# Attention and MLP in one kernel: plain float32 for the product of the last two weights, and the memory term begun in the middle of a pair step

## Chip, cores and metric

One core of a Trainium2 chip runs the whole program. The metric is device microseconds of one execution; the time of a kernel is the median of several.

## What is computed

Two parts follow each other. Causal attention over 4 batches of 8 heads (576 positions, 64 wide) is mixed with the readout of a memory, and its result, 2304 tokens of 512, goes through an MLP that has no nonlinearity between its last two weights:

```python
a = softmax(causal(q @ k.T / 8))            # per batch and head
mem_out = (phi(q) @ M_prev) / (phi(q) @ z_prev + 1e-6)
x = g * mem_out + (1 - g) * (a @ v)          # phi(x) = elu(x) + 1, g = sigmoid(beta)
h = (x @ w1) * (x @ w2)                      # 512 -> 1024
out = (h @ w3) @ w_out                       # 1024 -> 1024 -> 512
```

The weights of the MLP arrive as 64-bit floats; the kernel reads them as pairs of 32-bit words and builds float32 from them.

## The kernel before

Since nothing stands between w3 and w_out, the kernel multiplies these two first (W = w3 @ w_out, 1024 x 512) and applies W to h. `w_gen` (L419) makes W in 8 blocks of 128 rows, each a sum over 8 chunks of 128. The operands are split in a high and a low part, both in the fast matmul form (float32r); each chunk is three matmuls of 512 columns: high x high, high x low, low x high. ACT copies a block's result as its high part (`wH`, L427), DVE takes the low part (`wL`, L405).

Every weight is converted by one of 40 jobs of 512 columns (`conv_stages`): 8 of w_out, 16 of w3, 16 of w1 and w2 (W12 below). The stages of a job: `load` (SP issues a DMA; below job 24 one DMA of 1 MB serves two jobs, L306, from there 0.5 MB for one, L315), `scale` (ACT, L322), `join` (two DVE instructions, L326 and L327), `split` (ACT copies the high part, L332; POOL subtracts for the low part, L333). `conv_tick` runs one stage of three jobs, one behind the other; `tick_ok` says whether a further job may start, by how much of W is done.

The attention works on pairs of heads, 16 of them, four to a batch. `pair_step(p)` issues the operations of one pair in the order of the list `ORDER`: t1 to t5 and th are transposes of the softmax of this pair (L236, L257; ACT copies them out of PSUM, L267), s and e are scores (PE L195, L209, with a DVE instruction for mask and maximum, L179) and exponentials (ACT L217) of the next pair, n their norm (DVE L221, L222, L226), lv, lqn and lq are loads (v; qn and z; q and k). The memory term of a pair is: `mem_a` (ma, two ACT instructions, L135, L136), `mem_b` (mb, DVE L141 and POOL L143), `mem_c` (mc, four small DVE instructions, L148 to L154, and POOL L156), all three for the next pair, then `mem_t` (mt, five transposes L162 into the PSUM tile x and an ACT copy), and `mem_mm` (mm, L273 and L274, plain float32), which leaves its sum in x; `pv_mm` (L283) adds to it, and `fin` (ACT L293, DVE L294) takes x out. There is one buffer each for qn, z, mt and x.

F in the list is a slot of filler for PE: `Fill.slot` runs one or two conversion ticks (two in the first 13 slots of a filler) and as many steps of the MLP as the plan of even shares asks for. In the first batch the filler is `w_gen`, in the others the MLP of the batch before (`gemm1`, L455, L461, L464, L466, L467; `gemm2`, L475, L480), and the MLP of the last batch runs alone at the end. The list is the order of priority; an engine's queue is filled by readiness and priority, so an instruction that is ready can be issued ahead of its place. Each queue runs in order.

Big SBUF tiles: eight slots r0 to r7 (raw weights in r0 to r3, split w_out in r4 to r7, later split W12 in all), a ring of four g0 to g3, seven x tiles (split w3 uses x4 to x6 in the first batch).

Of the kernel before, what the change touches and what calls it, by code (L numbers as in the profile page):

```python
# [8 lines left out]
F32 = mybir.dt.float32  # L9
F32R = mybir.dt.float32r  # L10
# [7 lines left out]


ORDER = (  # L20
    "lv lqn t1 F "
    "t2 F "
    "mt t3a F "
    "th t3b F "
    "s321 F "
    "e3 F "
    "n3 t4a F "
    "e2 e1 t4b t5 F "
    "n2 s4 F "
    "e4 F "  # L30
    "mm s0 e0 n4 F "
    "pv ma lq F "
    "fin mb mc F "
).split()


def f32(ap):
    return ap.bitcast(F32)
# [3 lines left out]
def attention_moe_kernel(  # L42
# [13 lines left out]
    nc = tc.nc  # L56
    B, H, D, _, S = qkt.shape
    DM = H * D
    NF = w12.shape[0]
    NC = DM // 128  # L60
# [9 lines left out]
    big = pool("big")  # L70
    ring = pool("ring")
# [6 lines left out]
    x_p = pool("x")  # L78
    a_p = pool("a", 2)
    o_p = pool("o", 2)  # L80
# [46 lines left out]
    def load_m(b):  # L127
        src = m_prev[b].rearrange("d (j t) e -> d t j e", t=2)
        for a in range(2):
            nc.sync.dma_start(out=md[64 * a:64 * a + 64, :, 64 * a:64 * a + 64], in_=src[:, a])  # L130
# [164 lines left out]


    def conv_stages(k, src, dh, dl):
        n = dh.shape[1]
        box = {}

        def load():
            if k < 24:
                if k % 2 == 0:
                    t = big.tile([128, 4 * n], F32, tag=f"r{k // 2 % 4}", name="wst")
                    raws[k // 2] = t.bitcast(U32).rearrange("p (j n w) -> p j n w", j=2, w=2)
                    nc.sync.dma_start(out=t.bitcast(U32), in_=src.bitcast(U32))  # L306
                box["raw"] = raws[k // 2][:, k % 2]
                return
            if k < 32:
                t = ring.tile([128, 3 * n], F32, tag=f"g{2 + k % 2}", name="wst")  # L310
                box["p"] = t[:, 2 * n:3 * n]
            else:
                t = x_p.tile([128, 2 * S], F32, tag=f"x{4 + k % 3}", name="wst")
            box["raw"] = t[:, 0:2 * n].bitcast(U32).rearrange("p (n w) -> p n w", w=2)
            nc.sync.dma_start(out=t[:, 0:2 * n].bitcast(U32), in_=src.bitcast(U32))  # L315

        def scale():
            if k < 24:
                box["p"] = ring.tile([128, n], F32, tag=f"g{k % 4}", name="wp")
            if k >= 32:  # L320
                box["p"] = o_p.tile([128, n], F32, tag="o", name="wp")
            nc.scalar.activation(out=box["p"], in_=f32(box["raw"][:, :, 1]), func=ACTF.Prelu, scale=2.0 ** -111, alpha=-(2.0 ** 32))  # L322

        def join():
            p = box["p"].bitcast(U32)
            nc.vector.tensor_scalar(out=p, in0=p, scalar1=3, scalar2=None, op0=ALU.logical_shift_left)  # L326
            nc.vector.scalar_tensor_tensor(  # L327
                out=p, in0=box["raw"][:, :, 0], scalar=29, in1=p, op0=ALU.logical_shift_right, op1=ALU.bitwise_or
            )

        def split():
            nc.scalar.activation(out=dh(), in_=box["p"], func=ACTF.Copy)  # L332
            nc.gpsimd.tensor_tensor(out=dl(), in0=box["p"], in1=f32(dh()), op=ALU.subtract)  # L333

        return load, scale, join, split

    big_t = {}

    def part(key, alloc, a, o, n):
        def get():  # L340
            if key not in big_t:
                big_t[key] = alloc()
            return big_t[key][:, a, o:o + n]
        get.shape = [128, n]
        return get

    conv_jobs = []
    raws = {}

    def add_job(src, key, alloc, o):  # L350
        conv_jobs.append(conv_stages(len(conv_jobs), src, part(key, alloc, 0, o, 512), part(key, alloc, 1, o, 512)))

    def whole(tag):
        return lambda: big.tile([128, 2, 1024], F32R, tag=tag, name="wsp")

    def w3_half(m):
        return lambda: x_p.tile([128, 2, S], F32R, tag=f"x{4 + m % 3}", name="w3s")

    for j in range(8):
        add_job(w_out[j // 2], ("wo", j // 2), whole(f"r{j // 2 + 4}"), 512 * (j % 2))  # L360
    for m in range(16):
        add_job(w3t[m // 2], ("w3", m), w3_half(m), 0)
    for j in range(16):
        add_job(w12[j // 2][:, 512 * (j % 2):512 * (j % 2) + 512], ("w12", j // 2), whole(f"r{j // 2}"), 512 * (j % 2))
    NJ = len(conv_jobs)
    tick = [0]
    nload = [0]
    w_done = [0]
    limit = [28]

    def tick_ok():
        k = tick[0]
        if 10 <= k < 26 and w_done[0] < k - 12:
            return False
        return k < limit[0] and (k < 32 or w_done[0] == 16)

    def load_upto(k):
        while nload[0] < min(k, NJ):
            conv_jobs[nload[0]][0]()
            nload[0] += 1  # L380

    def conv_tick():
        k = tick[0]
        tick[0] += 1
        if 0 <= k - 2 < NJ:
            conv_jobs[k - 2][3]()
        if 0 <= k - 1 < NJ:
            conv_jobs[k - 1][2]()
        if k < 24:
            load_upto(min(24, 8 + k // 2 * 2))  # L390
        else:
            load_upto(k + 2)
        if k < NJ:
            conv_jobs[k][1]()

    def conv_upto(k):
        while tick[0] <= k + 2:
            conv_tick()


    def w_gen():
        box = {}

        def low(i):
            nc.vector.scalar_tensor_tensor(  # L405
                out=wL[i], in0=box.pop(i), scalar=2.0 ** -16, in1=f32(wH[i]), op0=ALU.mult, op1=ALU.subtract
            )

        for i in range(NF):
            ps = ps_m.tile([128, DM], F32, tag="m", name="m")  # L410
            n = 0
            for kc in range(8):
                m = 2 * i + kc // 4
                if kc % 4 == 0:
                    conv_upto(8 + m)
                w = big_t["w3", m]
                wo = big_t["wo", kc // 2].rearrange("p a (k e) -> p a k e", k=2)[:, :, kc % 2]
                for a, b in ((0, 0), (0, 1), (1, 0)):
                    nc.tensor.matmul(ps, lhsT=w[:, a, 128 * (kc % 4):128 * (kc % 4) + 128], rhs=wo[:, b], start=(n == 0), stop=(n == 23))  # L419
                    n += 1  # L420
                if kc % 4 == 3:
                    w_done[0] += 1
                yield 648
                if kc == 0 and i:
                    low(i - 1)
            with tc.high_priority(100):
                nc.scalar.activation(out=wH[i], in_=ps, func=ACTF.Copy, scale=2.0 ** -16)  # L427
            box[i] = ps
        low(NF - 1)
# [55 lines left out]
    def moe_gen(b):  # L485
        for n in (2 * b, 2 * b + 1):
            yield from gemm1(n)
            while 128 * (done_g[0] + 1) <= U * (n + 1):
                yield from gemm2(done_g[0])
                done_g[0] += 1  # L490

    MOE_NS = 2 * NF * 8 * 366 + 9 * 0.5 * NF * 648
    W_NS = NF * 8 * 648


    class Fill:
# [6 lines left out]
        def slot(self):  # L503
            self.n += 1
            for _ in range(self.ticks if self.n > SLOTS else 2):
                if tick[0] <= NJ + 1 and tick_ok():
                    conv_tick()
            goal = self.lead * self.total * max(0, self.n - self.wait) / (self.slots - self.wait)
            while self.live and self.spent < goal:
                self.step()  # L510
# [11 lines left out]
    SLOTS = sum(t[0] == "F" for t in ORDER)  # L522
# [72 lines left out]
    for c in (3, 2, 1):  # L595
        s_exp(0, c)
        conv_tick()
# [12 lines left out]
    for b in range(B):  # L610
        load_m(b)
        if b == 0:
            F = Fill(w_gen(), W_NS, SLOTS * NC, wait=4)
        else:
            limit[0] = NJ + 2
            F = Fill(moe_gen(b - 1), MOE_NS, SLOTS * NC)
        for j in range(NC):
            pair_step(b * NC + j, F)
        F.finish()
    F = Fill(moe_gen(B - 1), MOE_NS, 1)  # L620
# [34 lines left out]
```

## Time and profile before

| | us |
|---|---|
| median of 3 runs | 605.61 (605.23 to 606.65) |
| the profiled execution | 605.53 |
| its span, first to last instruction | 603.7 |
| PE busy in the span | 554.7 (92%) |
| DVE busy | 310.9 (51%) |
| ACT busy | 294.0 (49%) |
| POOL busy | 161.8 (27%) |

Busy shares are means over stages of different kinds: the first batch of pair steps (18.9 to 144.4 us) computes W, the next three (144.4 to 522.4) run the MLP of the batch before as filler, and the rest is the MLP of the last batch alone. A stage is read by itself, with the granted clock of PE beside it (1.00 is 2.4 GHz, 0.50 is 1.2).

### The profile page before, as it was taken

Reading aid. Unit: us, or ns where it says so; the run is one execution under the profiler, and the core shown is the slowest. Engines: PE = TensorE matmul, PEld = TensorE weight load, DVE = VectorE, ACT = ScalarE, POOL = GpSimd, SP = SyncE. Lnnn points to the kernel's source line nnn. Section 1 sums busy time; section 2 is a strip of 40 time slices with the busy share of each in tenths; the row PEclk is TensorE's granted clock in tenths of the full one; section 3 lists DMA queues with packets and bytes.
Section 4 is the critical chain, followed back from the end, with each engine's and each line's share of the span. In section 5 each row is a group of like instructions: output and inputs, shape, how many; then the busy total and the mean of one; then the engine's idle time right before and its main releaser. Section 6 shows DMA issues by size and latency. Waiting matters only on the chain.

```text
span 603.7 us, 9527 instructions
## 1 busy us (share of the span) xinstructions
PE 554.7 (92%) x3504; PEld 455.7 (75%) x3504; DVE 310.9 (51%) x910; ACT 294.0 (49%) x747; POOL 161.8 (27%) x177
## 2 busy tenths in 40 slices
PE   4388889979789999999899989998999999999997
PEld 2255666757668788878787878777887889898996
DVE  5999687387882818172718172726435451111111
ACT  4776567575774445454545353515453644130210
POOL 1565144135653213121312031202120221031220
PEclk9879799989979999999999999999999999999999
DMA  7576321358522120203020302030213000000001
GB/s 277 210 274 234 97 68 27 90 174 241 171 87 71 38 88 5 86 23 111 10 82 25 102 5 84 25 108 27 64 28 99 22 23 1 36 1 17 18 2 52
DMA packets 23070, 48.32 MB, mean 80 GB/s; under 512 B 6896, under 2 KB 13040, under 8 KB 21488
## 3 DMA queue, kind: packets, MB, share of 16 engines
q1 hardware_dynamic: 23024, 47.72, 24.3%
q8 instruction: 27, 0.44, 0.3%
q14 instruction: 19, 0.16, 0.1%
HBM read 43.00 MB, written 4.72 MB: 79 GB/s over the span
## 4 chain that ended last, share of the span: by engine, by line
PE 58%; DVE 14%; issue 8%; DMA 7%; ACT 7%; POOL 5%; SPq 0%; DVEq 0%; POOLq 0%; ACTq 0%
PE m L455 26%; PE m L475 13%; PE x L283 5%; PE s L236 4%; PE s L195 4%; DMA qn<-qn 3%; PE m L419 3%; DMA wst<-w 3%; DVE sm L226 3%; DVE sm L179 2%; DVE wp L327 2%; POOL e L143 2%; ACT sm L217 2%; DVE wp L326 2%; POOL wsp L333 1%
## 5 line engine op out<-in xcount | busy, mean ns | idle before, releaser
L455 PE MATMUL m<-xs,wsp 128*128 128x288 f32 x1536 | 232.0, 302 | 9.9 <-DVE a L464 5.8
L455 PEld LDWEIGHTS m<-xs,wsp 128*128 128x128 f32 x1536 | 209.2, 189 | 19.8 <-DVE a L464 7.6
L467 POOL TENSOR_TENSOR ht<-a,ht 128x288 fp32r<-128x288 f32 (+2 forms) x96 | 57.4, 611 | 287.1 <-ACT ht L466 267.5
L217 ACT ACTIVATE sm<-sm,mx 128x448 f32<-128x448 f32 (+2 forms) x144 | 83.1, 578 | 71.3 <-DVE mx L179 71.1
L475 PE MATMUL m<-wH,ht 128*128 128x512 f32 x288 | 98.4, 402 | 0.0
L464 DVE SCALAR_TENSOR_TENSOR a<-m,a 128x288 f32<-128x288 f32 x64 | 29.1, 455 | 114.8 <-PE m L455 114.6
L267 ACT ACTIVATE pt<-s 128x512 f32<-128x512 f32 (+1 forms) x144 | 66.1, 484 | 34.4 <-PE s L236 26.9
L236 PE MATMUL s<-ident,sm 128*128 128x128 f32 x448 | 69.4, 282 | 8.6 <-DVE sm L226 6.4
L226 DVE TENSOR_SCALAR sm<-sm,sums 128x448 f32<-128x448 f32 (+2 forms) x144 | 74.5, 558 | 1.5
L195 PE MATMUL s<-raw 64*128 64x288 f32 (+3 forms) x320 | 60.7, 474 | 12.9 <-ACT pt L267 5.3
L236 PEld LDWEIGHTS s<-ident,sm 128*128 128x128 f32 x448 | 56.3, 145 | 14.1 <-issue 6.8
L179 DVE CUSTOM_DVE_ANT_0 sm<-s,mask 128x448 f32<-128x448 f32 (+2 forms) x144 | 59.3, 447 | 11.4 <-PE s L195 10.8
L475 PEld LDWEIGHTS m<-wH,ht 128*128 128x128 f32 x288 | 54.1, 188 | 13.2 <-issue 2.6
L195 PEld LDWEIGHTS s<-raw 64*128 64x128 f32 x320 | 32.3, 199 | 35.6 <-issue 11.2
L466 ACT ACTIVATE ht<-a 128x288 fp32r<-128x288 f32 (+2 forms) x96 | 31.4, 357 | 53.5 <-DVE a L464 53.4
L419 PE MATMUL m<-wsp,w3s 128*128 128x512 f32 x192 | 56.1, 426 | 0.7 <-POOL w3s L333 0.7
L475 PE MATMUL m<-wL,ht 128*128 128x512 f32 x144 | 56.3, 391 | 0.0
L283 PE MATMUL x<-pt,v 128*64 128x448 f32 (+4 forms) x384 | 46.7, 392 | 0.0
L461 ACT ACTIVATE a<-m 128x288 f32<-128x288 f32 x64 | 26.0, 407 | 40.8 <-PE m L455 35.0
L283 PEld LDWEIGHTS x<-pt,v 128*64 128x64 f32 x384 | 25.0, 137 | 24.1 <-issue 19.1
L419 PEld LDWEIGHTS m<-wsp,w3s 128*128 128x128 f32 x192 | 35.0, 198 | 10.7 <-issue 2.5
L143 POOL TENSOR_TENSOR e<-qn,z 128x640 f32<-128x640 f32 x16 | 25.4, 1589 | 34.9 <-DVE qn L141 34.0
(63 smaller groups left out, 498.0 us busy)
## 6 DMA issues: line engine op xcount, KB each, us to landing
raw<-qkt SPq DMA_DIRECT2D x16, 576.0 KB, 3.8
wst<-w3t SPq DMA_DIRECT2D x8, 1024.0 KB, 7.5
wst<-w SPq DMA_DIRECT2D x16, 512.0 KB, 4.5
qn<-qn SPq DMA_DIRECT2D x16, 320.0 KB, 2.9
v<-v SPq DMA_DIRECT2D x32, 160.0 KB, 2.4
out<-o SPq DMA_DIRECT2D x18, 256.0 KB, 2.0
wst<-w_out SPq DMA_DIRECT2D x4, 1024.0 KB, 9.7
z<-z_prev SPq DMA_DIRECT2D x16, 64.0 KB, 2.9
```

Source lines behind the costliest of these rows:

```text
L143: nc.gpsimd.tensor_tensor(out=e, in0=t, in1=zb, op=ALU.mult)
L179: nc.vector.tensor_tensor_reduce(out=sm[a][c][:, lo:hi] if c else sm0[:, 0:64], in0=x, in1=mask[:, S - KE[c] + lo:S - KE[c] + hi] if c els ...
L195: nc.tensor.matmul(x[:, o:o + hi - lo], lhsT=t[r, 0, 128 * c - 64:128 * c + 64], rhs=t[r, 1, lo:hi], start=True, stop=True)
L217: nc.scalar.activation(out=x, in_=x, func=ACTF.Exp, bias=mx, scale=-1.0, accum_out=sums_of(p)[:, k:k + 1])
L226: nc.vector.tensor_scalar(out=x, in0=x, scalar1=sums_of(p)[:, k:k + 1], scalar2=None, op0=ALU.mult)
L236: tr = lambda o, c, a, kc: nc.tensor.transpose(ps[:, o:o + 128], sm[a][c][:, 128 * kc:128 * kc + 128], ident)
L267: nc.scalar.activation(out=d, in_=s, func=ACTF.Copy)
L283: nc.tensor.matmul(x[64 * a:64 * a + 64, 384 + q0:384 + q1], lhsT=vv[:, a, kc], rhs=pt[:, a, o:o + q1 - q0], start=False, stop=(q0 == 0 or ...
L419: nc.tensor.matmul(ps, lhsT=w[:, a, 128 * (kc % 4):128 * (kc % 4) + 128], rhs=wo[:, b], start=(n == 0), stop=(n == 23))
L455: nc.tensor.matmul(ps[:, 0:U], lhsT=w[:, i, x, j], rhs=x_t[NC * b + j][:, xx, U * u:U * u + U], start=(k == 0), stop=(k == 11))
L467: nc.gpsimd.tensor_tensor(out=hbuf(f, 1)[:, p:p + c], in0=a[:, o:o + c], in1=f32(hbuf(f, 0)[:, p:p + c]), op=ALU.subtract)
L475: nc.tensor.matmul(ps, lhsT=hbuf(f, a)[:, p:p + 128], rhs=b[f], start=(k == 0), stop=(k == 23))
```

## The change

The operands of W are no longer split. `split` does nothing below job 24, and the scaled and joined value is written straight to its place. A chunk of W is one plain float32 matmul of 512 columns. The planned cost of a chunk goes from 648 to 870 ns; the filler starts at slot 4 in place of 5.

Unsplit w_out takes r4 and r5, so raw weights have six slots (r0 to r3, r6, r7) and are loaded 12 jobs ahead in place of 8. Unsplit w3 goes into the ring, one tile for a block. W12 jobs stage in x4 to x6 and in an output tile (before, jobs 24 to 31 staged in the ring). `tick_ok` lets W3 jobs run up to four blocks ahead.

In the list, mt goes from slot 3 to the start of a step, lqn from slot 1 to slot 2 (behind mt), ma from slot 12 to 5, mb from 13 to 6, mc from 13 to 9.

```diff
 ORDER = (
-    "lv lqn t1 F "
-    "t2 F "
-    "mt t3a F "
+    "lv mt t1 F "
+    "lqn t2 F "
+    "t3a F "
     "th t3b F "
-    "s321 F "
-    "e3 F "
+    "s321 ma F "
+    "e3 mb F "
     "n3 t4a F "
     "e2 e1 t4b t5 F "
-    "n2 s4 F "
+    "n2 s4 mc F "
     "e4 F "
     "mm s0 e0 n4 F "
-    "pv ma lq F "
-    "fin mb mc F "
+    "pv lq F "
+    "fin F "
 ).split()
...
-                    t = big.tile([128, 4 * n], F32, tag=f"r{k // 2 % 4}", name="wst")
+                    t = big.tile([128, 4 * n], F32, tag=f"r{(0, 1, 2, 3, 6, 7)[k // 2 % 6]}", name="wst")
...
-            if k < 32:
-                t = ring.tile([128, 3 * n], F32, tag=f"g{2 + k % 2}", name="wst")
-                box["p"] = t[:, 2 * n:3 * n]
-            else:
-                t = x_p.tile([128, 2 * S], F32, tag=f"x{4 + k % 3}", name="wst")
+            t = x_p.tile([128, 2 * S], F32, tag=f"x{4 + k % 3}", name="wst")
...
-            if k < 24:
-                box["p"] = ring.tile([128, n], F32, tag=f"g{k % 4}", name="wp")
-            if k >= 32:
-                box["p"] = o_p.tile([128, n], F32, tag="o", name="wp")
+            box["p"] = dh() if k < 24 else o_p.tile([128, n], F32, tag="o", name="wp")
...
         def split():
+            if k < 24:
+                return
...
+    def wo_tile(j):
+        def alloc():
+            if j // 2 not in wo_t:
+                wo_t[j // 2] = big.tile([128, 2, 1024], F32, tag=f"r{4 + j // 2}", name="wo")
+            return wo_t[j // 2][:, j % 2]
+        return alloc
...
+        w3_tile = lambda i=m // 2: ring.tile([128, 1024], F32, tag=f"g{i % 4}", name="w3s")
...
         k = tick[0]
-        if 10 <= k < 26 and w_done[0] < k - 12:
-            return False
-        return k < limit[0] and (k < 32 or w_done[0] == 16)
+        if 8 <= k < 24:
+            return w_done[0] >= (k - 8) // 2 - 3
+        return k < limit[0] and (k < 32 or w_done[0] == NF)
...
-            load_upto(min(24, 8 + k // 2 * 2))
+            load_upto(min(24, 12 + k // 2 * 2))
...
-                for a, b in ((0, 0), (0, 1), (1, 0)):
-                    nc.tensor.matmul(ps, lhsT=w[:, a, 128 * (kc % 4):128 * (kc % 4) + 128], rhs=wo[:, b], start=(n == 0), stop=(n == 23))
-                    n += 1
-                if kc % 4 == 3:
-                    w_done[0] += 1
-                yield 648
+                nc.tensor.matmul(ps, lhsT=w[:, 128 * kc:128 * kc + 128], rhs=wo[:, 512 * (kc % 2):512 * (kc % 2) + 512], start=(kc == 0), stop=(kc == 7))
+                yield 870
...
+            w_done[0] += 1
...
-            F = Fill(w_gen(), W_NS, SLOTS * NC, wait=4)
+            F = Fill(w_gen(), W_NS, SLOTS * NC, wait=3)
```

## Rows read from the trace of the kernel before

**Rows 1.** Stages: from:to, us; busy us of PE, PEld, DVE, ACT, POOL; clock; DMA.

```profile
18.90:58.40 39.50, 29.30 (x141) 20.47 (x141) 39.04 (x82) 27.76 (x62) 22.60 (x15) 0.87 0.64 224
58.40:89.30 30.90, 25.43 (x131) 18.29 (x131) 23.67 (x66) 17.45 (x43) 9.88 (x7) 0.89 0.30 92
89.30:112.30 23.00, 21.07 (x116) 14.52 (x117) 16.34 (x55) 15.75 (x38) 8.08 (x6) 1.00 0.16 45
112.30:144.40 32.10, 28.91 (x155) 20.76 (x154) 22.65 (x59) 20.62 (x46) 11.58 (x9) 0.95 0.55 171
144.40:185.10 40.70, 34.12 (x210) 27.13 (x209) 32.13 (x72) 28.10 (x64) 22.55 (x18) 0.92 0.45 141
185.10:522.40 337.30, 330.77 (x2237) 277.86 (x2236) 153.76 (x508) 159.07 (x431) 68.52 (x88) 1.00 0.17 51
```

**Rows 2.** Waits of PE, 18.9 to 144.4: waiter, releaser: us, times, longest.

```profile
PE x L162 <- POOL qn L156: 7.1, 2, 5.6
...
PE s L195 <- ACT pt L267: 4.6, 3, 3.2
```

**Rows 3.** Stages as in rows 1, two stretches at half clock.

```profile
60.80:67.50 6.70, 4.31 (x16) 3.84 (x17) 4.51 (x9) 2.27 (x6) 1.30 (x1) 0.50 0.29 63
132.50:135.80 3.30, 3.30 (x9) 2.15 (x7) 3.08 (x12) 2.46 (x6) 1.56 (x2) 0.50 0.41 142
```

**Rows 4.** Stages, L326 on DVE alone: first and third pair step.

```profile
18.90:58.40 39.50, 9.22 (x12) 0.87 0.64 224
89.30:112.30 23.00, 1.27 (x3) 1.00 0.16 45
```

**Rows 5.** Stages, L327 on DVE alone: the same two steps.

```profile
18.90:58.40 39.50, 12.84 (x12) 0.87 0.64 224
89.30:112.30 23.00, 2.08 (x3) 1.00 0.16 45
```

**Rows 6.** Stages, L333 on POOL alone: the first step.

```profile
18.90:58.40 39.50, 17.89 (x12) 0.87 0.64 224
```

**Rows 7.** Timeline around 52.5: start, us, engine, line, what.

```profile
52.32 1.49 POOL L333 TENSOR_TENSOR w3s<-wp,w3s 128x512 fp32r<-128x512 f32 x1 [1.89 <-ACT w3s L332]
...
52.57 1.26 DVE L221 SCALAR_TENSOR_TENSOR sums<-sums,gis 128x2 f32<-128x2 f32 x1
```

**Rows 8.** Chain of work, third pair step: start, us, what.

```profile
104.51 2.29 PE m L419 x9
...
107.02 0.75 PE x L274 x2
```

**Rows 9.** Timeline of SP; then the page's DMA issues (KB, us to landing).

```profile
31.74 0.33 SPq L121 DMA_DIRECT2D qn<-qn  x1
...
32.66 20.40 SPq L306 DMA_DIRECT2D wst<-w3t  x6
...
qn<-qn SPq DMA_DIRECT2D x16, 320.0 KB, 2.9
```

**Rows 10.** Timeline of ACT in the fourth pair step.

```profile
130.78 0.67 ACT L322 ACTIVATE wst<-wst 128x512 f32<-128x512 f32 x1 [1.20 <-DMA wst<-w]
```

**Rows 11.** Timeline: mem_t after the first step (PE); L156 in steady state (POOL).

```profile
63.19 0.48 PE L162 MATMUL x<-ident,qn 128*128 128x128 f32 x1 [5.61 <-POOL qn L156]
...
232.91 1.44 POOL L156 TENSOR_TENSOR qn<-qn,n 128x640 f32<-128x640 f32 x1
```

**Rows 12.** Timeline: pv, fin's subtract and the next transposes, first and seventh step.

```profile
49.67 2.92 PE L283 MATMUL x<-pt,v 128*64 128x128 f32 x24
...
54.02 0.60 PE L236 MATMUL s<-ident,sm 128*128 128x128 f32 x4
...
58.40 0.75 DVE L294 TENSOR_TENSOR xs<-x,xs 128x576 fp32r<-128x576 f32 x1
...
246.00 0.76 DVE L294 TENSOR_TENSOR xs<-x,xs 128x576 fp32r<-128x576 f32 x1 [3.36 <-ACT xs L293]
...
248.08 0.60 PE L236 MATMUL s<-ident,sm 128*128 128x128 f32 x4
```

More of the change, by code (lines that the diff above doesn't have):

```diff
@@ L297, in conv_stages @@
     def conv_stages(k, src, dh, dl):
-        n = dh.shape[1]
+        n = 512
         box = {}
@@ L337, in attention_moe_kernel, with add_job, get @@
     big_t = {}
-    def part(key, alloc, a, o, n):
-        def get():
+    conv_jobs = []
+    raws = {}
+    def add_job(src, key, alloc, o, split):
+        def get(a):
             if key not in big_t:
                 big_t[key] = alloc()
[L343 to L357, printed above, removed]
+            t = big_t[key]
+            return t[:, a, o:o + 512] if split else t[:, o:o + 512]
+        conv_jobs.append(conv_stages(len(conv_jobs), src, lambda: get(0), lambda: get(1)))
+    wo_t = {}
+    def wo_tile(j):
[4 more added lines that the diff above has]
+        return alloc
     for j in range(8):
-        add_job(w_out[j // 2], ("wo", j // 2), whole(f"r{j // 2 + 4}"), 512 * (j % 2))
+        add_job(w_out[j // 2], ("wo", j // 2), wo_tile(j // 2), 512 * (j % 2), False)
     for m in range(16):
-        add_job(w3t[m // 2], ("w3", m), w3_half(m), 0)
+        w3_tile = lambda i=m // 2: ring.tile([128, 1024], F32, tag=f"g{i % 4}", name="w3s")
+        add_job(w3t[m // 2], ("w3", m // 2), w3_tile, 512 * (m % 2), False)
     for j in range(16):
-        add_job(w12[j // 2][:, 512 * (j % 2):512 * (j % 2) + 512], ("w12", j // 2), whole(f"r{j // 2}"), 512 * (j % 2))
+        w12_tile = lambda f=j // 2: big.tile([128, 2, 1024], F32R, tag=f"r{f}", name="wsp")
+        add_job(w12[j // 2][:, 512 * (j % 2):512 * (j % 2) + 512], ("w12", j // 2), w12_tile, 512 * (j % 2), True)
     NJ = len(conv_jobs)
@@ L396, in conv_upto @@
     def conv_upto(k):
-        while tick[0] <= k + 2:
+        while tick[0] <= k + (1 if k < 24 else 2):
             conv_tick()
@@ L410, in w_gen @@
             ps = ps_m.tile([128, DM], F32, tag="m", name="m")
-            n = 0
             for kc in range(8):
-                m = 2 * i + kc // 4
                 if kc % 4 == 0:
-                    conv_upto(8 + m)
-                w = big_t["w3", m]
-                wo = big_t["wo", kc // 2].rearrange("p a (k e) -> p a k e", k=2)[:, :, kc % 2]
-                for a, b in ((0, 0), (0, 1), (1, 0)):
-                    nc.tensor.matmul(ps, lhsT=w[:, a, 128 * (kc % 4):128 * (kc % 4) + 128], rhs=wo[:, b], start=(n == 0), stop=(n == 23))
-                    n += 1
-                if kc % 4 == 3:
-                    w_done[0] += 1
-                yield 648
+                    conv_upto(8 + 2 * i + kc // 4)
+                w = big_t["w3", i]
+                wo = big_t["wo", kc // 2]
+                nc.tensor.matmul(ps, lhsT=w[:, 128 * kc:128 * kc + 128], rhs=wo[:, 512 * (kc % 2):512 * (kc % 2) + 512], start=(kc == 0), stop=(kc == 7))
+                yield 870
                 if kc == 0 and i:
                     low(i - 1)
+            w_done[0] += 1
             with tc.high_priority(100):
@@ L492, in attention_moe_kernel @@
     MOE_NS = 2 * NF * 8 * 366 + 9 * 0.5 * NF * 648
-    W_NS = NF * 8 * 648
+    W_NS = NF * 8 * 870
     class Fill:
```

## Prediction, before the change was run

> **What bounds the kernel now.** I read the stages first, then who PE waits for, then single rows. The profiled execution took 605.53 us (span 603.7 and 1.8 around it), 0.1 under the median of 605.61; the sum is made from 605.5.
>
> The table of stages [rows 1] splits the span at the ends of pair steps. From 185.1 to 522.4, PE is busy 330.77 of 337.3 us at full clock: whatever the change does there must shorten PE's own work to be seen, and it removes none of it. The first batch, 18.9 to 144.4, is different. Its four steps take 39.5, 30.9, 23.0 and 32.1 us, with PE busy 29.30, 25.43, 21.07 and 28.91, and the clock at 0.87, 0.89, 1.00 and 0.95. That is 20.8 us of idle PE, and stretches at half clock, in the only stage in which the product W3 x W_out is computed. In its first step DVE is busy 39.04 of 39.5 us: DVE sets the pace there.
>
> PE's waits in that batch [rows 2] name, past the start, two places: mem_t waits for POOL's last multiply of the memory term (7.1 us, once 5.6), and a score matmul waits for ACT (4.6, once 3.2). Behind both PE runs at half clock [rows 3]: 4.31 us of work at 60.8 and 3.30 at 132.5, that is 2.2 and 1.7 us lost.
>
> **Why DVE is slow in the first step.** The join of a converted weight (L326, L327) takes 9.22/12 + 12.84/12 = 1.84 us there, and 1.27/3 + 2.08/3 = 1.12 in the third step [rows 4, 5]. In that first step 12 of POOL's 15 instructions are the low-part subtracts of L333, 17.89 of its 22.60 us [rows 1, 6]. Where both engines work, the DVE instruction ends when POOL's ends: L221 on 128x2 elements, started at 52.57, took 1.26 us beside a POOL subtract from 52.32 to 53.81 [rows 7]. So the subtracts cost DVE time, not only POOL's. The Trainium skill, "SBUF — State Buffer", section "Who interferes with whom", says the same more sharply: DVE's second port pair is GpSimd's only one, held as an exclusive lock for a whole instruction, and the loser blocks. By that rule the removed subtracts could free DVE by up to their whole 17.9 us in the first step (estimate); the joins show less, and the sum goes by the joins.
>
> **Part 1, plain float32 product: PE.** Each of 64 products was three matmuls on split operands: nine of them take 2.29 us in the chain, 0.763 per product [rows 8]. Plain float32 is already used by mem_mm: one 448-column product is two instructions and 0.75 us [rows 8], so 512 columns take 0.857. Extra: 64 x 0.094 = **+6.0 us**, on the path wherever PE is the bound. The lower end is 5 (a little more overlap of weight loads: 128 in place of 192); the upper is the planner's own change of price, 648 to 870 ns, 14.2 in all. I take the rows.
>
> **Part 2, no split of W_out and W3.** 24 of the 40 jobs lose their ACT copy and their POOL subtract, and PE no longer waits for either. ACT (27.76 of 39.5 busy in the worst step) and POOL bound nothing by themselves; what counts is DVE. 12 joins in the first step at 1.84 in place of 1.12 are 8.7 us, of which POOL's share due to L333 (17.89/22.60) is 6.9. Other DVE instructions are held too and not counted. Against it stands that more is converted early: counting the ticks of tick_ok by slot, the first step goes from job 4 to 15 before, 4 to 18 after: three more jobs, 3 x 1.12 = 3.4. Net **-4 us** with ends 0 (DVE is held by the memory term's own POOL work as before) and -8 (all held instructions counted).
>
> **Part 3, the buffers and the loads.** Converted W3 goes to the ring, W_out takes two big slots in place of four, so raw weights have six slots and are loaded 12 jobs ahead in place of 8. Before, SP issued the second W3 load only at 32.66, behind the qn load at 31.74, which waits for mem_t [rows 9]. After it, the qn load stands behind the loads of the first slot, two more of which find a free buffer; what is then queued behind it is jobs 16 on, needed in the second step. Cost 0. Jobs 24 to 27 (W12) move from the fourth step (tick count: slots 2 to 7) to the third (slots 3 to 7), and are staged in x tiles that nothing else uses in that batch. In the fourth step the stall of 3.2 us sat behind an ACT that waited for such a load [rows 10] and cost 1.7 of clock besides: **-4.8 us** if the load is early enough, 0 if the wait only moves to the third step.
>
> **Part 4, the order of the memory term.** mem_a, mem_b and mem_c move from slots 12 and 13 of a step to slots 5, 6 and 9; mem_t from slot 3 to the start, and the qn load behind it. In steady state this changes nothing: the last multiply L156 for the eighth pair ends at 234.35, 12 us before fin of the step ahead of it [rows 11, 12], though the list has mem_c behind fin: what was ready was issued ahead of its place. Two ACT instructions ahead of e3, one DVE ahead of n3, and two on POOL each fill waits there, 0; if the cover is gone (the qn load landing late), ACT holds e3 back for the 2.9 us that such a load takes [rows 9], once or twice in the first batch. Where DVE is late, in the first step, PE stood still for 5.6 us until L156 released mem_t at 63.19 [rows 11], and lost 2.2 us of clock after it [rows 3]. With the chain ahead of most norms in the list, this stall goes: **-7.8 us**, ends 0 and -7.8. What is late next is fin, see the first rival.
>
> Moved mem_t costs nothing in steady state: fin's DVE subtract ends at 246.76 and the step's first transposes, in whose place mem_t now stands, start at 248.08 [rows 12].
>
> **Sum:** 6.0 - 4 - 4.8 - 7.8 = -10.6; 605.5 - 10.6 = **595 us**. Ends: 605.5 + 14.2 = 620 if nothing is gained; 605.5 + 5 - 8 - 4.8 - 7.8 = 590 if all is, without the W12 stage.
>
> **Rivals.**
> 1. *mem_t waits for fin (slower).* mem_t writes the PSUM tile that fin reads, and PE takes its queue in order. At the end of the first step fin's subtract sat in DVE's queue until 59.15, while PE had got to the next step's transposes at 54.02 [rows 12]: with mem_t in front, PE would stand 5.1 us, in place of the 5.6 it stands now, and, as an estimate, half of that at each of the next two ends of steps in the batch. If DVE is not relieved, parts 2 and 4 give nothing: 605.5 + 6.0 - 4.8 + 5.1 = 612. It decides as soon as DVE takes longer from pv to fin than PE's filler does (1.4 us there, from 52.59 to 54.02). For it: DVE at 99% in that step. Against: 24 subtracts less. Chance 0.14.
> 2. *A plain product costs four passes at today's price.* 4/3 of 0.763 is 1.017 per product: 64 x 0.254 = 16.3 in place of 6.0, and the time is 605. The Trainium skill, "FP8 and Floating Point Precision", section "TensorE Precision Notes", gives this count: true FP32 takes four passes through the array. The trace agrees on the count (two instructions, each at half rate) but at 0.857, since today's three passes carry exposed weight loads [rows 8]. Chance 0.07.
> 3. *The stage of the W12 conversion gains too.* 144.4 to 185.1 has 6.6 us of idle PE and clock 0.92 [rows 1]; if the backlog of joins at its start and the tighter staging were to blame, up to the idle time goes: 589. Against: its twelve remaining jobs still split. Chance 0.16.
> 4. *The waits only move* (ACT's wait for the W12 load into the third step, less relief of DVE): 605.5 + 6 - 2 - 7.8 = 602. Chance 0.10.
>
> **Chances and range.** Forecast 0.53, by itself 591 to 599; the rest as above. Under 0.2% (1.2 us) a measurement of this kernel cannot be told from no change. Faster: 0.53 + 0.16 + 0.10 = 0.79; same 0.07; slower 0.14. The range reaches from 585 (rival 3 with the ends of part 2) to 606 (rivals 2 and 4), leaving out rival 1 and a little below.
>
> **What would show it.** L419 with 128 matmuls at about 0.86 us per product; L333 with 16; L326 and L327 in the first step near 0.42 and 0.69; no PE wait over 1 us at mem_t in the first two steps; the first batch's end near 134 in place of 144.4; from there a trace like the one before. Wrong would be: waits of L162 on L294 of several us (rival 1), products near 1.0 us (rival 2), joins in the first step still near 1.8 (part 2), or a step from 185 on that is longer by more than 0.3 us.

## Result and the profile after

The changed kernel takes 592.75 us (592.14 to 593.40) against 606.13 of the kernel before on the same chip: ratio 0.978 (0.976 to 0.980), 13.4 us less. The forecast was 595, 10.6 less. Time and direction were right; the stages from which the time came are in part others.

The table of stages of the kernel after, cut again at the ends of pair steps (the steps of the first batch, the W12 stage, the steady stage; from:to, length, busy us of PE, PEld, DVE, ACT, POOL, then the clock):

```profile
17.00:54.30 37.30, 30.39 (x112) 16.34 (x112) 32.04 (x93) 21.04 (x52) 5.85 (x4) 0.81 0.78 298
54.30:84.70 30.40, 26.57 (x118) 13.79 (x118) 23.63 (x67) 20.38 (x46) 8.01 (x6) 1.00 0.46 151
84.70:113.90 29.20, 26.56 (x114) 14.57 (x115) 23.91 (x62) 19.08 (x44) 8.04 (x6) 0.94 0.42 138
113.90:140.40 26.50, 26.50 (x120) 13.88 (x119) 16.21 (x52) 14.99 (x37) 5.72 (x4) 1.00 0.26 82
140.40:177.60 37.20, 32.76 (x216) 27.69 (x215) 21.97 (x60) 21.30 (x52) 15.10 (x13) 0.91 0.27 79
177.60:509.40 331.80, 330.85 (x2246) 278.90 (x2245) 149.12 (x507) 159.28 (x431) 66.77 (x87) 1.00 0.17 52
```

Against [rows 1]: the first step ends 4.1 us sooner (54.3 for 58.4), the second is 0.5 shorter, the third 6.2 *longer*, the fourth 5.6 shorter, the W12 stage 3.5 and the steady stage 5.5 shorter; the tail is 81.3 in both. Those sum to -13.0, the difference of the spans (603.7 and 590.7). So the first batch, in which I had placed all of the gain, gave 4.0 us (it ends at 140.4 for 144.4, not near 134); 9.0 came behind it.

PE's waits up to 141 us in the kernel after, past the start, to be held against [rows 2]:

```profile
PE x L162 <- DVE xs L294: 4.7, 2, 3.5
...
PE s L195 <- ACT pt L267: 2.1, 2, 1.7
...
PE x L162 <- POOL qn L156: 1.5, 1, 1.5
```

mem_t no longer waits 5.6 us for the memory term's POOL multiply; it waits up to 3.5 for fin's subtract in its place, at the end of the second step, and behind that wait PE again runs at half clock:

```profile
86.00:89.40 3.40, 3.40 (x13) 2.26 (x11) 1.73 (x2) 2.00 (x5) 1.54 (x2) 0.50 0.48 154
```

### The profile page after: what moved, and what is told of

The parts are those of the page before. It is cut to its first block, busy times and chain, and to the rows that moved or that the text cites. A ratio compares the mean times of both kernels' runs of the same rounds, so it can differ in the third digit from the quotient of the medians.

```text
span 590.7 us, 9323 instructions
## 1 busy us (share of the span) xinstructions
PE 557.9 (94%) x3440; PEld 441.2 (75%) x3440; DVE 288.5 (49%) x910; ACT 279.7 (47%) x723; POOL 125.5 (21%) x153
## 4 chain that ended last, share of the span: by engine, by line
PE 77%; DVE 11%; ACT 6%; POOL 2%; DMA 2%; issue 2%; SPq 0%; DVEq 0%; ACTq 0%
PE m L447 31%; PE m L467 17%; PE x L283 7%; PE s L236 7%; PE m L413 6%; PE s L195 6%; PE x L274 2%; ACT sm L217 2%; DVE sm L179 2%; DVE sm L226 2%; PE x L162 1%; POOL e L143 1%; DVE qn L141 1%; DMA wst<-w_out 1%; DVE wp L320 1%
## 5 line engine op out<-in xcount | busy, mean ns | idle before, releaser
L456 DVE SCALAR_TENSOR_TENSOR a<-m,a 128x288 f32<-128x288 f32 x64 | 29.1, 455 | 97.3 <-PE m L447 97.2
L179 DVE CUSTOM_DVE_ANT_0 sm<-s,mask 128x448 f32<-128x448 f32 (+2 forms) x144 | 58.4, 448 | 22.1 <-PE s L195 20.5
L236 PEld LDWEIGHTS s<-ident,sm 128*128 128x128 f32 x448 | 56.8, 146 | 16.0 <-issue 12.5
L413 PE MATMUL m<-wo,w3s 128*128 128x512 f32 x128 | 66.0, 635 | 1.7 <-DVE w3s L320 1.7
L467 PEld LDWEIGHTS m<-wH,ht 128*128 128x128 f32 x288 | 54.1, 188 | 13.4 <-issue 2.6
L195 PE MATMUL s<-raw 64*128 64x288 f32 (+3 forms) x320 | 56.2, 455 | 8.0 <-DMA raw<-qkt 4.4
L226 DVE TENSOR_SCALAR sm<-sm,sums 128x448 f32<-128x448 f32 (+2 forms) x144 | 62.4, 476 | 1.8
L458 ACT ACTIVATE ht<-a 128x288 fp32r<-128x288 f32 (+2 forms) x96 | 31.2, 356 | 56.8 <-DVE a L456 56.8
L195 PEld LDWEIGHTS s<-raw 64*128 64x128 f32 x320 | 30.6, 191 | 32.3 <-issue 11.7
L283 PEld LDWEIGHTS x<-pt,v 128*64 128x64 f32 x384 | 25.1, 137 | 25.7 <-issue 21.1
L453 ACT ACTIVATE a<-m 128x288 f32<-128x288 f32 x64 | 25.8, 404 | 37.9 <-PE m L447 32.2
L413 PEld LDWEIGHTS m<-wo,w3s 128*128 128x128 f32 x128 | 22.7, 200 | 20.0 <-issue 17.6
```

Source lines behind the costliest of these rows:

```text
L179: nc.vector.tensor_tensor_reduce(out=sm[a][c][:, lo:hi] if c else sm0[:, 0:64], in0=x, in1=mask[:, S - KE[c] + lo:S - KE[c] + hi] if c els ...
L195: nc.tensor.matmul(x[:, o:o + hi - lo], lhsT=t[r, 0, 128 * c - 64:128 * c + 64], rhs=t[r, 1, lo:hi], start=True, stop=True)
L226: nc.vector.tensor_scalar(out=x, in0=x, scalar1=sums_of(p)[:, k:k + 1], scalar2=None, op0=ALU.mult)
L236: tr = lambda o, c, a, kc: nc.tensor.transpose(ps[:, o:o + 128], sm[a][c][:, 128 * kc:128 * kc + 128], ident)
L283: nc.tensor.matmul(x[64 * a:64 * a + 64, 384 + q0:384 + q1], lhsT=vv[:, a, kc], rhs=pt[:, a, o:o + q1 - q0], start=False, stop=(q0 == 0 or ...
L413: nc.tensor.matmul(ps, lhsT=w[:, 128 * kc:128 * kc + 128], rhs=wo[:, 512 * (kc % 2):512 * (kc % 2) + 512], start=(kc == 0), stop=(kc == 7))
```

## Experiments

Lines of the kernel after: L413 is W's product (L419 before), L319 and L320 the join, L327 and L328 the split (W12 only), L315 the scale, L456 the DVE instruction and L453 the ACT copy that empty the MLP's PSUM tiles (L464 and L461 before).

### The two halves of the change apart

The new list on the kernel before, nothing else:

```diff
 ORDER = (
-    "lv lqn t1 F "
+    "lv mt t1 F "
...
-    "pv ma lq F "
-    "fin mb mc F "
+    "pv lq F "
+    "fin F "
```

> The kernel before with the new order list alone (weights still split). Theory A, from the two traces: the steady stage lost its PE idle time (6.5 us before, 0.9 after) because of the order, so this kernel's steady stage is 5 to 6 us shorter, and the first batch gains 2 to 6 us at mem_t; time 594 to 599. Theory B, as predicted: the order changes nothing in steady state (stage stays at 337 us) and gains only at mem_t of the first step; time 598 to 605.

600.8 us (598.3 to 602.1), ratio 0.991 (0.988 to 0.994): as a total in the range of theory B (598 to 605). The old list on the changed kernel:

```diff
 ORDER = (
-    "lv mt t1 F "
+    "lv lqn t1 F "
...
-    "pv lq F "
-    "fin F "
+    "pv ma lq F "
+    "fin mb mc F "
```

> The changed kernel with the old order list (unsplit weights, new buffers, new ticks). Theory A: the first batch and the W12 stage keep some 7 us of gain less what the memory term's late end costs (0 to 5), the steady stage stays at 337; time 598 to 603. Theory B: the whole gain is the weights'; time 592 to 594.

595.5 us (593.4 to 597.2), ratio 0.982 (0.978 to 0.985). Their steady stages, first the new list on the old kernel, then the old list on the new one, the latter with its W12 stage ahead of it:

```profile
184.40:515.20 330.80, 329.00 (x2229) 276.83 (x2228) 148.99 (x508) 159.06 (x430) 66.83 (x87) 1.00 0.17 51
```

```profile
140.10:174.50 34.40, 30.85 (x213) 26.71 (x212) 19.80 (x61) 21.70 (x52) 15.76 (x13) 0.95 0.25 79
174.50:514.10 339.60, 332.57 (x2245) 279.12 (x2244) 153.62 (x507) 159.54 (x431) 67.35 (x87) 1.00 0.16 50
```

The steady stage follows the list and not the weights: 330.8 and 331.8 with the new one, 337.3 and 339.6 with the old one. (All ten kernels of this record that have the new list in that stage take 330.5 to 332.2 us for it.) Theory A of the first run holds there, and "the order changes nothing in steady state" is refuted. Ahead of that stage the new list gave the old kernel little: the first batch ends at 142.1 for 144.4, and the W12 stage takes 42.3 for 40.7. Total and stage don't agree for the second run either: it lies between its two theories, under 598 to 603, since the old list does better where the new one was to help, ahead of the steady stage (that stage begins at 174.5 with the old list, 177.6 with the new one). The first batches end alike (140.1 and 140.4); the difference is in the W12 stage, 34.4 us at a clock of 0.95 for 37.2 at 0.91. The list gives 6 to 8 us in the steady stage and, on the new weights, costs 3 before it.

### One slot for mem_t

On the kernel after:

```diff
-    "lv mt t1 F "
-    "lqn t2 F "
+    "lv t1 F "
+    "mt lqn t2 F "
```

> The changed kernel with mem_t one slot later, behind t1 and its filler (the qn load behind it). Theory A: the 3.5 us for which PE waits at mem_t for fin's subtract at the end of the second step is covered by t1 and a slot (1.5 us) or more, and the half clock after it goes: 588 to 591. Theory B: fin is late because ACT and DVE work on pulled-ahead W12 jobs, and PE then waits just as long at the next instruction: 592 to 594.

590.2 us (588.0 to 591.1), ratio 0.973 (0.971 to 0.976): as A forecast in total, and only in part for A's reason. At the end of the second step PE still waits 2.2 us for fin's subtract, and the half clock behind it stays (0.94 in the third step). The steady stage begins 7.2 us sooner, at 170.4, half of it won in the first batch and half in the W12 stage, and takes 336.9 us:

```profile
82.40:109.00 26.60, 24.91 (x108) 13.22 (x109) 21.56 (x62) 18.95 (x44) 8.94 (x6) 0.94 0.53 170
...
170.40:507.30 336.90, 331.02 (x2245) 278.91 (x2245) 148.36 (x508) 158.55 (x431) 66.79 (x87) 1.00 0.16 51
```

Five waits of PE of 0.9 to 1.4 us, some 60 us apart, make up the extra 5.1. One of them in the timeline (start, us, engine, what):

```profile
270.80 1.53 POOL L143 TENSOR_TENSOR e<-qn,z 128x640 f32<-128x640 f32 x1 [1.81 <-DVE qn L141]
...
272.37 0.82 DVE L148 TENSOR_REDUCE n<-e 128x10 f32<-128x640 f32 x1 [1.65 <-POOL e L143]
...
275.55 0.45 DVE L456 SCALAR_TENSOR_TENSOR a<-m,a 128x288 f32<-128x288 f32 x1
...
276.06 1.47 PE L447 MATMUL m<-xs,wsp 128*128 128x288 f32 x9 [1.42 <-DVE a L456]
```

mem_c's reduce stands in DVE's queue and holds it for 1.65 us, until POOL has multiplied; behind it queue the score maxima and L456, for which PE waits. Three of the five (3.5 of the 5.9 us) go through ACT: L453 stands there behind exponentials that wait for the same maxima. In the kernel after, the chain starts a slot sooner, and of such waits one of 0.8 us is left in the whole stage.

### The reduce's wait taken away

On that kernel, the multiply moved from POOL to DVE, so that the reduce waits for nobody:

```diff
-        nc.gpsimd.tensor_tensor(out=e, in0=t, in1=zb, op=ALU.mult)
+        (nc.gpsimd if p < 5 else nc.vector).tensor_tensor(out=e, in0=t, in1=zb, op=ALU.mult)
```

> The kernel with the later mem_t in all steps, and from the sixth pair on mem_b's multiply on DVE in place of POOL. Theory A: the steady stage's waits come from mem_c's reduce, which holds DVE's queue while POOL multiplies, ahead of the score maxima and of the MLP's product; with the multiply on DVE nothing waits there and the stage goes from 336.9 to 332 to 334: 585 to 588. Theory B: the waits are DVE's load at that place, which the multiply raises: 590 or more.

586.4 us (585.3 to 587.2), ratio 0.967 (0.965 to 0.969). The steady stage:

```profile
169.00:502.60 333.60, 331.35 (x2245) 278.95 (x2244) 157.59 (x517) 159.11 (x432) 52.36 (x77) 1.00 0.17 51
```

DVE works 9.2 us more and the stage is 3.3 us shorter; PE's idle time falls from 5.9 to 2.3 us. As A has it, it is the wait in DVE's queue and not DVE's load; the 2.3 us that are left are six waits of at most 0.6 us for L456 and L453.

### POOL beside DVE

The removed subtract put back into `split` of the kernel after, as work that nobody waits for:

```diff
             if k < 24:
+                nc.gpsimd.tensor_tensor(out=wL[NF - 1], in0=box["p"], in1=box["p"], op=ALU.subtract)
                 return
```

> The changed kernel with one POOL subtract of 128x512 per W_out and W3 job put back, which nothing waits for (it writes zeros into a tile that the last block's low part overwrites later). Theory A: POOL's reads hold DVE; the joins of the first step go from 1.2 back towards 1.8 us, that step is 3 to 6 us longer; time 596 to 600. Theory B: the gain comes from the shorter chain of a job alone, and POOL beside it costs nothing: 592 to 594.

604.0 us (602.5 to 604.7), ratio 0.996 (0.995 to 0.998): 11 us slower than the kernel after, more than either theory said. Its first step (the same 93 DVE instructions):

```profile
17.00:60.40 43.40, 30.91 (x112) 16.41 (x112) 42.16 (x93) 20.62 (x50) 23.44 (x19) 0.79 0.67 256
```

L319 and L320 alone in that step, one row each:

```profile
17.00:60.40 43.40, 11.49 (x15) 0.79 0.67 256
...
17.00:60.40 43.40, 13.22 (x15) 0.79 0.67 256
```

In the kernel after, the same two lines in its first step of 37.3 us:

```profile
17.00:54.30 37.30, 7.29 (x15) 0.81 0.78 298
...
17.00:54.30 37.30, 11.07 (x15) 0.81 0.78 298
```

A join takes 1.65 us for 1.22, and DVE as a whole 42.16 for 32.04: 15 POOL instructions more (17.6 us of POOL) cost DVE 10.1 us, of which the joins hold 6.4. Nearly all of the rest is in three more lines: L226, the scaling of the exponentials, takes 2.4 us more, L154 0.8 and L141 0.5. First L226 of the kernel after, then of this one:

```profile
17.00:54.30 37.30, 5.51 (x13) 0.81 0.78 298
...
17.00:60.40 43.40, 7.95 (x13) 0.79 0.67 256
```

Other DVE instructions were not held, also beside a POOL subtract: the reduce L148 took 0.81 us in both kernels, once beside a subtract from 22.38 to 23.42, and the score maxima L179 are unchanged too. The step is 6.1 us longer, the two behind it 2.9 and 1.4.

The other way in which this POOL work could cost time is POOL's own queue, in which the memory term's multiplies now stand behind it. PE's waits up to 151 us say how much that is (in the kernel after the same two are 4.7 and 1.5 us):

```profile
PE x L162 <- DVE xs L294: 8.3, 2, 4.7
...
PE x L162 <- POOL qn L156: 2.3, 1, 2.3
```

The wait for POOL grew by 0.8 us, PE's waits for DVE by 7.3 in sum.

### What the product costs on PE

Every second chunk left out of W, all conversions kept; half of each sum of W is missing:

```diff
+                if kc % 2 == 0:
-                nc.tensor.matmul(..., start=(kc == 0), stop=(kc == 7))
+                    nc.tensor.matmul(..., start=(kc == 0), stop=(kc == 6))
```

> The changed kernel with every second chunk of W left out (32 of 64 float32 products, 27 us of PE less, all conversions kept). Theory A: PE bounds the first batch from its second step on; the batch is 15 to 20 us shorter: 573 to 578. Theory B: conversion on DVE and ACT bounds it, and PE's product was mostly beside it: under 8 us shorter, 585 to 591.

573.6 us (two executions), ratio 0.945 (0.940 to 0.951), theory A. The first step is 1.6 us shorter, and the first batch ends at 122.7 for 140.4: 17.7 us for 27.4 us of PE work. A product's PE time counts for two thirds on the path, nearly nothing of it in the first step. The price itself, in the chain of the kernel after:

```profile
121.16 1.72 PE m L413 x4
...
129.42 0.86 PE m L413 x2
...
134.80 0.75 PE x L274 x2
```

Two instructions a product, 0.86 us, as forecast from L274.

### The W12 jobs that came early

The staging tiles of W12 are now free from the start, and the loads run ahead of their place: three are issued at 56.8, in the second step, by SP,

```profile
56.81 1.38 SPq L311 DMA_DIRECT2D wst<-w  x3
```

and the subtracts of W12 spread over steps two to four and the W12 stage like this (POOL, L328):

```profile
54.30:84.70 30.40, 5.18 (x4) 1.00 0.46 151
84.70:113.90 29.20, 5.17 (x4) 0.94 0.42 138
113.90:140.40 26.50, 2.93 (x2) 1.00 0.26 82
140.40:177.60 37.20, 8.21 (x6) 0.91 0.27 79
```

I had put only jobs 24 to 27 ahead of the W12 stage. First the jobs from 29 on were held back:

```diff
             t = x_p.tile([128, 2 * S], F32, tag=f"x{4 + k % 3}", name="wst")
+            if k >= 29:
+                nc.vector.tensor_copy(out=t[:, 0:1], in_=f32(wH[NF - 1])[:, 0:1])
```

> The changed kernel with the W12 jobs from 29 on held back to the second batch (one column of W's last block is copied into the staging tile ahead of the load, which then has to wait for it). Theory A: pulled-ahead jobs make fin late in the second step and cost the first batch its gain; it ends at 135 to 138 in place of 140.4, and the W12 stage takes 40 to 42 us in place of 37.2; time 592 to 595. Theory B: pulling ahead is free for the first batch, which ends at 140 again, and only the W12 stage grows: 595 to 598.

596.7 us (595.6 to 597.5), ratio 0.983 (0.979 to 0.987). The first batch ends at 137.8, 2.6 sooner, as A has it, but the W12 stage takes 44.8, 7.6 more, and the total is B's: the cost of holding back is larger than both said, and the 3.5 us at mem_t stayed. Then all of them:

```diff
+            nc.vector.tensor_copy(out=t[:, 0:1], in_=f32(wH[NF - 2])[:, 0:1])
...
-    limit = [28]
+    limit = [24]
```

> The changed kernel with all W12 jobs held back to the last eighth of the first batch (a column of W's seventh block is copied into the staging tile ahead of each load, and ticks stop at job 24). Theory A: jobs 24 to 28 in ACT's queue ahead of fin are what makes mem_t wait 3.5 us at the end of the second step; the wait falls under 1 us, the first batch ends at 133 to 137, and the W12 stage grows by 8 us or more: 594 to 602. Theory B: fin is late there by DVE's and ACT's other work, the wait stays over 2.5 us.

599.9 us (596.8 to 600.6), ratio 0.987 (0.982 to 0.992), theory A. Second to fourth step and W12 stage:

```profile
53.60:78.60 25.00, 24.07 (x114) 13.15 (x115) 17.99 (x57) 15.33 (x37) 2.81 (x2) 1.00 0.15 44
78.60:105.20 26.60, 26.41 (x119) 13.87 (x118) 14.98 (x52) 13.74 (x35) 2.79 (x2) 1.00 0.17 51
105.20:136.90 31.70, 27.68 (x124) 14.46 (x122) 18.09 (x59) 16.26 (x40) 5.77 (x5) 1.00 0.44 139
136.90:187.00 50.10, 41.67 (x239) 35.47 (x239) 40.81 (x89) 31.18 (x70) 24.78 (x21) 0.83 0.44 144
```

Without W12 jobs the second step takes 25.0 in place of 30.4, with no wait at mem_t at its end, and the third 26.6 in place of 29.2; the wait comes back with the jobs, at the end of the fourth step (4.9 us). The W12 stage pays 12.9 us. So the early jobs cost the first batch 3.5 us in all and give more than three times that back behind it. How they delay fin is seen at the end of the second step of the kernel after (ACT, POOL, DVE and PE):

```profile
80.58 1.29 ACT L327 ACTIVATE wsp<-wp 128x512 fp32r<-128x512 f32 x2 [0.90 <-DVE wp L320]
...
81.29 2.49 POOL L328 TENSOR_TENSOR wsp<-wp,wsp 128x512 fp32r<-128x512 f32 x2 [5.40 <-ACT wsp L327]
...
82.59 0.67 ACT L315 ACTIVATE wp<-wst 128x512 f32<-128x512 f32 x1 [0.71 <-POOL wsp L328]
...
83.16 0.63 ACT L293 ACTIVATE xs<-x 128x576 fp32r<-128x576 f32 x1
...
84.10 0.69 DVE L320 SCALAR_TENSOR_TENSOR wp<-wst,wp 128x512 uint32<-128x512 uint32 x1
84.71 0.75 DVE L294 TENSOR_TENSOR xs<-x,xs 128x576 fp32r<-128x576 f32 x1
...
85.61 0.98 PE L162 MATMUL x<-ident,qn 128*128 128x128 f32 x5 [3.51 <-DVE xs L294]
```

pv ended at 79.3. ACT's queue holds two copies of W12 that wait for a join, and a scale that waits until POOL has left its output tile, ahead of fin's copy at 83.16; on DVE a W12 join holds fin's subtract for another 0.9 us, to 84.71.

### The raw slots

```diff
-tag=f"r{(0, 1, 2, 3, 6, 7)[k // 2 % 6]}"
+tag=f"r{k // 2 % 4}"
...
-            load_upto(min(24, 12 + k // 2 * 2))
+            load_upto(min(24, 8 + k // 2 * 2))
```

> The changed kernel with four raw slots and eight jobs of lead, as before. Theory A, as predicted for the buffers: 0, time 592 to 593.5. Theory B: W3 loads wait behind the qn load again and the first step grows by 2 to 5 us: 594.5 to 598.

594.5 us (593.6 to 596.9), ratio 0.980 (0.976 to 0.984). Not told apart from the kernel after by the intervals. The total is at the edge of B's range, but not for B's reason: in its profile the first step is not longer but shorter (34.3 us), at full clock throughout, and the next two are 1.9 and 1.4 longer. The buffers by themselves are worth 0 to 2 us.

### Versions that beat both

mem_t a slot later where it waits for fin, at the start where it gives the steady stage its time:

```diff
+EARLY = (
+    "lv t1 F "
+    "mt lqn t2 F "
...
-        for t in ORDER:
+        for t in EARLY if p < 5 else ORDER:
```

> The changed kernel with mem_t one slot later in the first five pair steps alone, and at the start of the step in the others. Theory A: the two effects seen apart add up, a stage up to 170 as with the later mem_t and a steady stage of 331.8 as with the early one: 585 to 587. Theory B: the steady stage's waits hang on the whole history, and it stays at 335 to 337: 589 to 591.

585.1 us (584.2 to 586.4), ratio 0.965 (0.961 to 0.969), theory A; the W12 stage and the steady stage:

```profile
137.20:168.90 31.70, 28.80 (x213) 25.09 (x212) 23.16 (x60) 21.05 (x52) 15.41 (x13) 1.00 0.28 87
168.90:501.10 332.20, 331.07 (x2246) 278.95 (x2245) 149.17 (x507) 159.31 (x432) 66.90 (x87) 1.00 0.17 52
```

Both effects add up, and the W12 stage runs at full clock. Two attempts, on this kernel with two lists, on the 2.2 us that mem_t still waits at the end of the second step:

```diff
+        with tc.high_priority(100):
             nc.scalar.activation(out=t[:, 0], in_=x, func=ACTF.Copy)
             nc.vector.tensor_tensor(out=t[:, 1], in0=x, in1=f32(t[:, 0]), op=ALU.subtract)
```

> The kernel with two orders, and fin's two instructions given priority over what is queued within 100 places ahead of them. Theory A: at the end of the second step fin is late only because ACT has the W12 jobs 24 to 28 queued ahead of it (they wait for a join or a POOL subtract); with priority PE's wait of 2.2 us at mem_t goes: 582 to 584. Theory B: ACT's queue is not the cause and the wait stays: 585 to 586.

583.7 us (582.8 to 584.6), ratio 0.963 (0.960 to 0.965). The wait stayed at 2.2 us, and ACT's queue at that place stands in the same order as without the priority. So A's number came without its reason, and the run says nothing on the cause; the totals overlap those of the kernel with two lists (584.2 to 586.4).

```diff
 EARLY = (
     "lv t1 F "
-    "mt lqn t2 F "
-    "t3a F "
+    "t2 F "
+    "mt lqn t3a F "
```

> The kernel with two orders, with mem_t at slot 3 in the first five steps in place of slot 2. Theory A: the 2.2 us wait for fin at the end of the second step is covered by one more slot, and nothing else waits there: 582 to 584. Theory B: what stands behind mem_t (the qn load, then the memory term of the next pair) becomes late in its turn: 585 to 588.

584.9 us (583.6 to 585.6), ratio 0.963 (0.958 to 0.968): the wait falls to 0.9 us, and the W12 stage takes 33.3 in place of 31.7:

```profile
136.40:169.70 33.30, 30.80 (x213) 26.66 (x212) 20.66 (x61) 21.35 (x52) 15.79 (x13) 0.95 0.26 82
```

Nothing is won in total, and not for B's reason: behind the first step PE waits at most 0.2 us for the memory term. The W12 stage has PE busy 2.0 us longer, at a clock of 0.95 for 1.00, though its one long wait of PE is shorter (2.4 us for 2.9). Why the clock fell here and not there was not found.

## Why the prediction was right, and where not

- **What bounds the kernel.** Right for the first batch: DVE in the first step (half of the products gone, and that step is 1.6 us shorter), PE mostly from the second on. Wrong that the steady stage could only be changed by PE's own work: its 6.5 us of idle PE [rows 1] were waits for the two instructions that empty the MLP's tiles, and went. In the kernel before, from 185 us on:

```profile
PE m L455 <- DVE a L464: 4.4, 5, 1.7
PE m L455 <- ACT a L461: 2.2, 3, 1.7
```

- **Part 1, +6.0.** The price of a product is right (0.86 for 0.857). On the path it counts for 17.7/27.4, so the term is nearer to 4 (an estimate from that run). Rival 2, four passes at the old price, is out.
- **Part 2, -4, too small.** Putting the POOL work back costs 11 us. Against that stand the 6.9 that I had for the joins, from which 3.4 for three more jobs were taken off. The three more jobs came (15 joins, at 1.22 us each and not 1.12). I priced the joins and noted that other held instructions are not counted; they are over a third of DVE's loss (3.7 of 10.1). So the term was some 4 us too small, an estimate from that run. That the DVE instruction ends when POOL's ends [rows 7] holds for some instructions only: the reduce and the maxima were not held. The rule of the Trainium skill's page "SBUF — State Buffer", section "Who interferes with whom", gave 17.9 us as an upper bound (an estimate). For 17.6 us of POOL in the first step DVE lost 10.1, between that and the joins' share (6.9) and nearer to the latter.
- **Part 3, 0 and -4.8.** The fourth step lost its stall as said (5.6 us shorter, no idle PE). The step that failed is that jobs 24 to 27 move from the fourth step to the third: with free staging tiles, W12 jobs ran ahead of every tick, from the second step on, and ten of the sixteen were through ahead of the W12 stage. That is my own sentence on steady state (what is ready is issued ahead of its place), not applied here. The third step became 6.2 us longer, but not by these jobs alone: without them it still takes 26.6. PE is busy 5.5 us longer in it; 1.7 of that is the half clock at 86.0, and more of W's products fall into this step. First the products there before (L419), then after (L413):

```profile
89.30:112.30 23.00, 10.92 (x40) 6.93 (x41) 1.00 0.16 45
...
84.70:113.90 29.20, 15.44 (x30) 5.35 (x31) 0.94 0.42 138
```

The W12 stage became 3.5 us shorter. So rivals 4 and 3 came true, both in part.

- **Part 4, -7.8 at mem_t.** The stall at the end of the first step and the half clock behind it went (1.2 us of wait in place of 5.6, full clock from 54.3 to 84.7). But it goes with the old list as well (0.9 us on the changed kernel) and with the old weights (0.6): either half of the change removes it, so it can't be put down to the order alone. On the old weights it came with a first batch only 2.3 us shorter, not 7.8. In the changed kernel most came back one step later: 3.5 us of wait, and 1.7 of clock behind it.
- **Part 4, 0 in steady state.** Wrong: -5.5. That L156 ended 12 us early [rows 11] showed that the chain was in time, not that it stood well in DVE's queue.
- **Rival 1.** Its wait is there, which I had named as a sign of being wrong: 3.5 us at the end of the second step, with another holder. ACT's queue is full of W12 work, and DVE's W12 joins add 0.9 us; it is not DVE's backlog of joins from the first step.
- **The sum.** -10.6 was forecast and -13.4 measured, 2.8 apart, and that they are so near is in part luck: errors of both signs cancel. By stage, the first batch was to give 10.6 and gave 4.0; what lay behind it was to give nothing and gave 9.0. By cause, the list was to give 7.8 and the weights with their buffers 2.8; alone, the list gave 5.3 and the weights 10.5, and together less than the two added up.

## To carry to other kernels

An instruction that waits for another engine holds all that is queued behind it on its own: look at what stands behind each wait of an off-path engine, also in a stage where the bound engine is 98% busy. POOL work beside DVE can be paid in DVE time, also if nobody needs POOL's result; see which DVE instructions are held (here joins and scalings, not the reduce or the maxima). Freeing a buffer lets loads and conversions run ahead of their place in the list; price where they land.

## Of the hardware, not expected

Up to the end of the first step the kernels ran for very different times at half clock (0.50, that is 1.2 GHz): 10.2 us in the kernel before, 20.5 in the kernel after, none in the kernel with four raw slots, whose first step is the shortest of the changed kernel's kind, 34.3 us for 37.3. One such stretch in the kernel after, with PE busy for 7.02 of its 10.2 us:

```profile
24.60:34.80 10.20, 7.02 (x13) 3.24 (x13) 9.71 (x19) 3.36 (x7) 1.30 (x1) 0.50 0.93 315
```

Ahead of it PE had waited 4.8 us at 12.3 and 3.3 us at 21.1, in both cases for DVE's scaling. The kernel with four raw slots waited nearly as long (4.5 and 3.3 us) and kept full clock. What decided between these cases was not found; up to 3 us of the first step (an estimate from 34.3 and 37.3), and so of the differences between the variants, may hang on it.
